# Turning probabilities in two halves of the array's rows, and an opening in which the products of w3 and w_out reach over steps 0 to 3

## The chip, the core and the metric

One core of one Trainium2 chip runs the kernel. Its engines run side by side, each through its own queue in order: TensorE (PE, with PEld for its loads of weights), VectorE (DVE), ScalarE (ACT), GpSimd (POOL) and SyncE (SP), which issues the DMAs. The metric is device time in microseconds (us), lower is better.

## What is computed

Banded attention with a few global keys, and a feed-forward part on its output:

```python
# attention, 4 batches, 8 heads, 768 positions, head size 64, n_global = 8, n_local = 96
scores = q @ k.T / 8 + bias        # bias = -slope(head) * distance
keep = (key < n_global) | ((0 <= row - key) & (row - key < n_local))
a = softmax(where(keep, scores, -1e9))
x = (a @ v) laid out as 3072 x 512
# feed-forward: w1, w2 are 512 x 1024, w3 is 1024 x 1024, w_out is 1024 x 512
out = (((x @ w1) * (x @ w2)) @ w3) @ w_out
```

The weights arrive as 64-bit numbers and are turned to 32 bits on the chip.

## The kernel before

**Steps.** The 4 batches are cut into 12 column blocks `c` of 256 positions, the 8 heads into 4 pairs. A step `s` handles two pairs of heads of one block; there are 24 steps, two for each `c`. A block that begins a batch (`c` divisible by 3: steps 0, 1, 6, 7, 12, 13, 18, 19) has less to do, and is called *first* here; the other steps are *full*.

- `visit(s)`: TensorE makes the values of step s-1 (`values`, L468) and the scores of step s (`scores`, L405), both in tiles of 64 rows by 64 columns of the array. Values go to two tiles `uu` of the pool `ps_v`, which has two PSUM banks. ScalarE copies one (L503), VectorE adds the other (L504), and the sum is split into a high and a low part, `xh` on ScalarE (L63) and `xl` on VectorE (L64).
- `rows` (L420, L421): VectorE adds the bias and finds the extreme of each row, ScalarE takes exp, eight times a step. `softmax` (L426 to L435) divides by the sum; in the opening ScalarE does all eight scalings (`scale(s)`, L433), and this call also issues the loads of step s+1 (`loads`, `qr` and `vr`).
- `turn(s, i)` for the two pairs: TensorE transposes the probabilities through the same two banks (`flip`, L445, L447), ScalarE copies each bank out to `ph` (L449, an *eviction*).
- `FeedForward.run`: the feed-forward of one stretch of x, as a generator. One call of `slices(1)` runs it to its next `yield`. The function takes a width: the first two blocks are run at 256 columns each, all later ones in pairs at 512. A slice is six matmuls of 512 columns, or twelve of 256. A pair of blocks at 512 takes 48 slices (32 for w1 and w2, L161 to L163, 16 for the product, L178 to L180); a single block at 256 takes 16 + 8.

**The opening.** w3 and w_out are multiplied once at the start: `fold(f, k...)` (L142), eight products for each of the eight blocks `f` of w3, each product two matmuls of 512 columns; then `low(f)` (L147) takes the low part of the sum. `w3(f)` and `w12(f)` bring a block of w3, or of w1 and w2: two DMAs into staging tiles, a conversion of three VectorE operations each (`convert`, L54, L56, L58), for w1 and w2 a copy on ScalarE (L122) and a low part on VectorE (`lows`, L130). The staging tile `raws` holds two pieces, `stage` four.

**What sets the order.** TensorE runs in the order of the code. In `first_steps` VectorE and SP do so as well, and the scheduler places ScalarE; in the later steps ScalarE is in code order and the scheduler places the other two. `SLICES` says how many slices stand ahead of, between and behind the two turnings of a step: (4, 4, 2) in steps 3 to 5, (4, 2, 2) in 6 and 7, (5, 4, 3) from 8 on. So 46 of the first 48 slices have run when step 8 begins.

Of the kernel before, what the change touches and what calls it, by code (L numbers as in the profile page):

```python
# [10 lines left out]
F32 = mybir.dt.float32  # L11
# [9 lines left out]
P = 128  # L21
# [45 lines left out]
class FeedForward:  # L67
# [29 lines left out]
    def weights(self, *names):  # L97
# [3 lines left out]
        for kind, *at in names:  # L101
            if kind == "w":
                f, n = divmod(at[0], 2)

                raw = self.stage[{3: 0, 5: 2, 6: 0}[f] + n] if f in (3, 5, 6) else self.raws[:, n]
                dst, src = self.t3s[:, at[0] % 4], self.src[n][f]
                fresh.append((n, f, dst.bitcast(F32).rearrange("p (i m) -> p i m", i=NCC)))
            elif kind == "o":
                dst, src = self.wo[:, at[0]], self.w_out[at[0]]
            else:  # L110
                f, z = at
                dst = self.mp.tile([P, PC], I32, tag=self.next(0, "agagoo"), name=f"t3_{f}_{z}")
                src = self.w3t[f, :, z * PC:(z + 1) * PC]
                self.t3[f, z] = dst
# [210 lines left out]
def banded(ctx, tc, ff, ns, nt, nf, oki, ident, qk, vx):  # L325
# [111 lines left out]

    def flip(c, hp, j, pr):

        first = c % NCB == 0 and j == 0  # L440
        nk = 1 if first else 2

        pt = ps_v.tile([P, 2, 2, P], F32, tag="v", name=f"t_{c}_{hp}_{j}")
        for u in range(2):
            nc.tensor.transpose(pt[:, u, 0], pr[:, j, u, BW:UW], ident)  # L445
            if not first:
                nc.tensor.transpose(pt[:, u, 1], pr[:, j, u, 0:P], ident)  # L447
        ph = at.tile([P, 2, 2, P], F32, tag="ph", bufs=4, name=f"ph_{c}_{hp}_{j}")
        nc.scalar.activation(ph[:, :, :nk], pt[:, :, :nk], AF.Copy)  # L449
        return ph  # L450

    def values(uu, c, hp, vr, phs):


        lo, hi, both = slice(0, HQ), slice(HQ, P), slice(0, P)
        for j, ph in enumerate(phs):
            own, win = (j, 0), (2 * NQ - 1 - j, 1)
            if c % NCB == 0 and j == 0:
                seqs = [[(own, r, both, True, True)] for r in (lo, hi)]
            else:  # L460
# [3 lines left out]
            for parts in zip(*seqs):  # L464
                for u in range(2):
                    rows = slice(u * D, (u + 1) * D)
                    for r, ((i, k), keys, q, start, stop) in enumerate(parts):
                        nc.tensor.matmul(uu[r][rows, j * P:][:, q], lhsT=vr[keys, i, rows], rhs=ph[keys, u, k, q], start=start, stop=stop)  # L468

# [20 lines left out]
    def visit(s):  # L490
        if s:
# [4 lines left out]
            for i, p in enumerate(pairs(s - 1)):  # L496
                values([x[:, i] for x in uu], *p, vrs[s - 1][i], phs[s - 1][NQ * i:NQ * (i + 1)])
        ps = [scores(*p, t) for p, t in zip(pairs(s), qrs[s])] if s < n else []
        if s:
# [5 lines left out]
            split(nc, *(x[:, h0:h0 + STEP] for x in xc), v)  # L505
            if h0 + STEP == NP and c < 2:
                work.append(ff.run(c, *xc, c * T, T))
            elif h0 + STEP == NP and c % 2:
                work.append(ff.run(c, *x2, (c - 1) * T, W))
# [5 lines left out]
    def turn(s, i, prs):  # L515

        phs.setdefault(s, []).extend(flip(*pairs(s)[i], j, prs[i][0]) for j in range(NQ))

    def first_steps():
# [43 lines left out]

        def fold_and_turn(f, s):
            ff.fold(f, 0, 1, 2, 3)
            turn(s, 0, prs)
            ff.fold(f, 4, 5, 6)
            turn(s, 1, prs)
            ff.fold(f, 7)

        w3(3)
        scale(0)
        ff.low(0)
        w3(4)
        ff.low(1)
        ff.low(2)
        w3(5)
        w12(0)
        fold_and_turn(3, 0)
        ff.lows()  # L580
        w3(6)
# [24 lines left out]
        prs = all_rows(3, visit(3))
        w12(6)
        slices(2)
        scale(3)
        ff.lows()  # L610
        w12(7)
        slices(SLICES[3][0] - 2)
        ff.lows()
        for i in range(STEP):
            turn(3, i, prs)
            slices(SLICES[3][i + 1])
        fits(nc, ff.mp, nf, oki)


    SLICES = [()] * 3 + [(4, 4, 2)] * 3 + [(4, 2, 2)] * 2 + [(5, 4, 3)] * (n - 8)  # L620
    with tc.manual_schedule(engines={mybir.EngineType.PE}):
        with tc.manual_schedule(engines={mybir.EngineType.DVE, mybir.EngineType.SP}):
            first_steps()
        with tc.manual_schedule(engines={mybir.EngineType.Activation}):
            for s in range(4, n + 1):
                rs = all_rows(s, visit(s))
# [6 lines left out]
                loads(s + 1)  # L633
                slices(SLICES[s][0] - 2)
                for i in range(STEP):
                    turn(s, i, rs)
                    slices(SLICES[s][i + 1])
            slices(10 ** 6)
# [45 lines left out]
```

## Time and profile before

| | |
|---|---|
| median of 3 runs | 591.76 us (591.63 to 592.16) |
| the profiled execution | 591.84 us |
| its span, first to last instruction | 589.8 us |
| TensorE busy | 565.4 us, 96% of the span |
| ScalarE busy | 297.3 us, 50% |
| VectorE busy | 274.2 us, 46% |
| mean granted clock of TensorE | 0.993 |
| share of TensorE in the chain that ended last | 82% (VectorE 13%, ScalarE 2%, DMA 2%) |

Matmuls overlap in the records, so the mean duration of one is longer than the time between the starts of two; for TensorE the document goes by starts.

### The profile page before, as it was taken

What the parts mean: (1) busy time and instruction counts of PE and PEld (TensorE: products, weight loads), DVE (VectorE), ACT (ScalarE), POOL (GpSimd) and SP (SyncE); (2) the same over time, 40 slices, a digit from 0 to 9 for tenths busy, and PEclk for the clock granted to TensorE, in tenths of its full rate; (3) what the DMA queues carried; (4) which work ended last, traced back from release to release, by engine and by line L of the source; (5) the groups of instructions that cost most, each with busy time, mean ns of one, the idle gap of its engine ahead of it and who ended that gap; (6) DMA issues with size and microseconds to landing.
All of it is one profiled execution on the core that took longest, in us unless ns stands there. A gap on an engine that the chain in (4) does not pass through costs nothing.

```text
span 589.8 us, 12652 instructions
## 1 busy us (share of the span) xinstructions
PE 565.4 (96%) x5216; PEld 452.0 (77%) x5216; DVE 274.2 (46%) x875; ACT 297.3 (50%) x801; POOL 1.3 (0%) x10
## 2 busy tenths in 40 slices
PE   2998996999999999999999999999999999999995
PEld 0444556989988888888888888888888888888884
DVE  8999999524444445404534432552244354022200
ACT  3065688446666456536646545663555565322210
POOL 0000000000000000000000000000000000000000
PEclk9999997999999999999999999999999999999999
DMA  8896754202223202212210330221232020100001
GB/s 300 306 359 239 224 217 148 82 21 82 65 80 116 67 15 81 64 55 82 81 57 24 102 114 18 66 64 35 82 116 79 2 82 1 54 19 1 0 36 41
DMA packets 23252, 54.19 MB, mean 92 GB/s; under 512 B 2705, under 2 KB 4753, under 8 KB 23185
## 3 DMA queue, kind: packets, MB, share of 16 engines
q1 hardware_dynamic: 23184, 53.29, 26.6%
q8 instruction: 43, 0.70, 0.5%
q14 instruction: 25, 0.20, 0.1%
HBM read 46.99 MB, written 6.29 MB: 90 GB/s over the span
## 4 chain that ended last, share of the span: by engine, by line
PE 82%; DVE 13%; ACT 2%; DMA 2%; issue 1%; DVEq 0%; ACTq 0%
PE m L161 15%; PE m L162 15%; PE m L163 15%; PE o L178 8%; PE o L179 7%; PE o L180 7%; PE v L468 5%; PE s L405 4%; PE t L445 3%; PE t L447 3%; DVE pr L420 2%; DVE t L58 1%; DVE t L56 1%; DVE t3s L56 1%; DMA stage<-w3t 1%; DVE t3s L58 1%
## 5 line engine op out<-in xcount | busy, mean ns | idle before, releaser
L421 ACT ACTIVATE pr<-pr,mx 128x232 f32<-128x232 f32 (+1 forms) x192 | 88.3, 461 | 23.4 <-DVE mx L420 21.6
L171 DVE TENSOR_TENSOR g<-m,a 128x512 f32<-128x512 f32 x48 | 33.0, 687 | 132.0 <-PE m L163 128.6
L161 PE MATMUL m<-xh,w2h 128*128 128x512 f32 (+1 forms) x224 | 84.4, 377 | 0.0
L161 PE MATMUL m<-xh,w1h 128*128 128x512 f32 (+1 forms) x224 | 81.6, 364 | 0.0
L162 PE MATMUL m<-xl,w1h 128*128 128x512 f32 (+1 forms) x224 | 81.0, 362 | 0.0
L163 PE MATMUL m<-xh,w1l 128*128 128x512 f32 (+1 forms) x224 | 81.0, 361 | 0.0
L162 PE MATMUL m<-xl,w2h 128*128 128x512 f32 (+1 forms) x224 | 80.8, 361 | 0.0
L163 PE MATMUL m<-xh,w2l 128*128 128x512 f32 (+1 forms) x224 | 80.7, 360 | 0.0
L178 PE MATMUL o<-wh,gh 128*128 128x512 f32 x192 | 77.0, 401 | 0.0
L179 PE MATMUL o<-wl,gh 128*128 128x512 f32 x192 | 75.1, 391 | 0.0
L180 PE MATMUL o<-wh,gl 128*128 128x512 f32 x192 | 74.9, 390 | 0.0
L142 PE MATMUL w<-wo,t 128*128 128x512 f32 x128 | 60.6, 623 | 13.1 <-DVE wo L58 11.1
L449 ACT ACTIVATE ph<-t 128x512 f32<-128x512 f32 (+1 forms) x96 | 49.8, 557 | 44.2 <-PE t L447 29.5
L504 DVE TENSOR_TENSOR vs<-v,vs 128x512 f32<-128x512 f32 x24 | 16.6, 690 | 117.2 <-ACT vs L503 117.2
L63 ACT ACTIVATE gh<-g 128x512 fp32r<-128x512 f32 x48 | 30.3, 630 | 68.1 <-DVE g L171 68.1
L142 PEld LDWEIGHTS w<-wo,t 128*128 128x128 f32 x128 | 24.3, 198 | 42.5 <-issue 24.2
L420 DVE CUSTOM_DVE_ANT_0 pr<-s,biasw 128x232 f32<-128x232 f32 x160 | 54.9, 394 | 0.0
L168 ACT ACTIVATE a<-m 128x512 f32<-128x512 f32 x48 | 28.4, 591 | 45.0 <-PE m L163 45.0
L161 PEld LDWEIGHTS m<-xh,w2h 128*128 128x128 f32 x224 | 42.3, 189 | 8.7 <-issue 2.6
L161 PEld LDWEIGHTS m<-xh,w1h 128*128 128x128 f32 x224 | 43.0, 192 | 6.6 <-DVE t3s L58 0.2
L445 PE MATMUL t<-ident,pr 128*128 128x128 f32 x192 | 43.0, 278 | 5.3 <-ACT pr L433 5.2
L162 PEld LDWEIGHTS m<-xl,w1h 128*128 128x128 f32 x224 | 43.0, 192 | 6.4
(84 smaller groups left out, 800.5 us busy)
## 6 DMA issues: line engine op xcount, KB each, us to landing
qr<-qk SPq DMA_DIRECT2D x32, 312.0 KB, 4.4
vr<-vx SPq DMA_DIRECT2D x32, 256.0 KB, 3.5
stage<-w3t SPq DMA_DIRECT2D x15, 512.0 KB, 6.8
out_dram<-ot SPq DMA_DIRECT2D x24, 256.0 KB, 2.0
raws<-w SPq DMA_DIRECT2D x10, 512.0 KB, 6.1
qr<-qk SPq DMA_DIRECT2D x16, 260.0 KB, 4.1
vr<-vx SPq DMA_DIRECT2D x16, 192.0 KB, 3.7
stage<-w SPq DMA_DIRECT2D x6, 512.0 KB, 7.1
```

The costliest lines, as they stand in the source:

```text
L142: nc.tensor.matmul(ps, lhsT=self.t3[f, z][:, i * P:(i + 1) * P].bitcast(F32), rhs=self.wo[:, k].bitcast(F32), start=k == 0, stop=k == NFC - 1)
L161: nc.tensor.matmul(ps[:, z], lhsT=mh, rhs=xh[:, i], start=i == 0, stop=False)
L162: nc.tensor.matmul(ps[:, z], lhsT=mh, rhs=xl[:, i], start=False, stop=False)
L163: nc.tensor.matmul(ps[:, z], lhsT=ml, rhs=xh[:, i], start=False, stop=i == NCC - 1)
L171: nc.vector.tensor_tensor(out=g, in0=ps, in1=a, op=ALU.mult)
L178: nc.tensor.matmul(ps, lhsT=gh[:, f, ts], rhs=self.wh[:, f], start=f == 0, stop=False)
L179: nc.tensor.matmul(ps, lhsT=gh[:, f, ts], rhs=self.wl[:, f], start=False, stop=False)
L180: nc.tensor.matmul(ps, lhsT=gl[:, f, ts], rhs=self.wh[:, f], start=False, stop=f == NFC - 1)
L420: nc.vector.tensor_tensor_reduce(out=pr[:, j, u, w0:], in0=ps[u][:, j, w0:UW], in1=bias, scale=-SCALE, scalar=3.0e38, op0=ALU.add, op1=ALU ...
L421: nc.scalar.activation(pr[:, j, u, w0:], pr[:, j, u, w0:], AF.Exp, bias=m, scale=-1.0, accum_out=sm[:, j, u:u + 1])
L445: nc.tensor.transpose(pt[:, u, 0], pr[:, j, u, BW:UW], ident)
L449: nc.scalar.activation(ph[:, :, :nk], pt[:, :, :nk], AF.Copy)
```

## The change

Two things change together.

**Turning.** `flip` now handles a whole pair of heads. Each transpose of 128 by 128 becomes two of 64 rows, one in the upper and one in the lower half of the array's rows (tiles of 64 rows by 128 columns), with 64 moving columns each, into two tiles of `ps_v`, one for each half. So each tile holds half of the positions of both `j`. An eviction is still 128x512, or 128x128 and 128x256 where the step is a first one; `values` picks the tile by the half that it needs, and its only 128-column matmuls are cut in two.

**Opening.** The first two blocks are run as a pair at 512 columns like the others, so the first slices come in step 4 instead of step 3. The products of w3 and w_out are spread by hand around the turnings of steps 0 to 3 (`around`), the conversions of w1 and w2 come later, and their staging tiles are dealt anew. Steps 4 to 7 now have 10, 12, 12 and 12 slices, again 46 of 48 when step 8 begins.

```diff
@@ weights @@
-                raw = self.stage[{3: 0, 5: 2, 6: 0}[f] + n] if f in (3, 5, 6) else self.raws[:, n]
+                raw = self.stage[{2: 0, 4: 2, 5: 0}[f] + n] if f in (2, 4, 5) else self.raws[:, n]
@@ flip @@
-        pt = ps_v.tile([P, 2, 2, P], F32, tag="v", name=f"t_{c}_{hp}_{j}")
-        for u in range(2):
-            nc.tensor.transpose(pt[:, u, 0], pr[:, j, u, BW:UW], ident)
-            if not first:
-                nc.tensor.transpose(pt[:, u, 1], pr[:, j, u, 0:P], ident)
-        ph = at.tile([P, 2, 2, P], F32, tag="ph", bufs=4, name=f"ph_{c}_{hp}_{j}")
-        nc.scalar.activation(ph[:, :, :nk], pt[:, :, :nk], AF.Copy)
+        halves = [slice(g * HQ, (g + 1) * HQ) for g in range(2)]
+        pts = [ps_v.tile([P, NQ, 2, 2, HQ], F32, tag="v", name=f"t{g}_{c}_{hp}") for g in range(2)]
+        for j in range(NQ):
+            for u in range(2):
+                for k, cols in enumerate((slice(BW, UW), slice(0, P))[:1 if first and j == 0 else 2]):
+                    for q, pt in zip(halves, pts):
+                        nc.tensor.transpose(pt[:, j, u, k], pr[q, j, u, cols], ident[q, q])
+        phs = [at.tile([P, NQ, 2, 2, HQ], F32, tag="ph", bufs=4, name=f"ph{g}_{c}_{hp}") for g in range(2)]
+        for ph, pt in zip(phs, pts):
+            if first:
+                nc.scalar.activation(ph[:, 0, :, 0], pt[:, 0, :, 0], AF.Copy)
+                nc.scalar.activation(ph[:, 1], pt[:, 1], AF.Copy)
+            else:
+                nc.scalar.activation(ph, pt, AF.Copy)
@@ visit @@
-            if h0 + STEP == NP and c < 2:
-                work.append(ff.run(c, *xc, c * T, T))
-            elif h0 + STEP == NP and c % 2:
+            if h0 + STEP == NP and c % 2:
                 work.append(ff.run(c, *x2, (c - 1) * T, W))
@@ later steps @@
-    SLICES = [()] * 3 + [(4, 4, 2)] * 3 + [(4, 2, 2)] * 2 + [(5, 4, 3)] * (n - 8)
+    SLICES = (5, 4, 3)
-            for s in range(4, n + 1):
+            for s in range(5, n + 1):
```

The new order in `first_steps`, behind `w3(3)`, `scale(0)` and `ff.low(0)`:

```python
ff.low(2)
w3(4)
ff.low(1)
around(0, [(3, 0, 1)], [(3, 2, 2)], [(3, 3, 4)])
w3(5)
prs = all_rows(1, visit(1))
ff.fold(3, 5, 6, 7)
ff.weights(("w", 0))
ff.low(3)
scale(1)
ff.weights(("w", 1))
around(1, [(4, 0, 4)], [(4, 5, 5)], [(4, 6, 7)])
ff.lows()
w3(6)
prs = all_rows(2, visit(2))
ff.low(4)
scale(2)
w12(1)
around(2, [(5, 0, 7), (6, 0, 0)], [(6, 1, 1)], [(6, 2, 3)])
ff.lows()
ff.low(5)
w3(7)
w12(2)
prs = all_rows(3, visit(3))
ff.lows()
scale(3)
w12(3)
around(3, [(6, 4, 7), (7, 0, 3)], [(7, 4, 5)], [(7, 6, 7)])
ff.lows()
ff.low(6)
w12(4)
ff.lows()
ff.low(7)
prs = all_rows(4, visit(4))
w12(5)
slices(2)
scale(4)
ff.lows()
slices(SLICES[0] - 2)
w12(6)
turn(4, 0, prs)
slices(2)
ff.lows()
slices(SLICES[1] - 2)
w12(7)
turn(4, 1, prs)
slices(SLICES[2] - 2)
ff.lows()
```

`around(s, a, b, e)` runs the products of list `a`, the first turning of step s, list `b`, the second turning, list `e`; (3, 0, 1) stands for the products 0 to 1 of block 3.

How the built programs differ, at three places. On TensorE, the first turning of step 0: `w_360` and `w_340` are the sums of block 3, `pr` the probabilities, `t` the tile they are turned into. Before:

```order
L142 MATMUL w_360<-wo,t_3_0_297 128x512 x4
L445 MATMUL t_0_0_365<-ident,pr_0_266 128x128 x2
L445 MATMUL t_0_1_370<-ident,pr_0_266 128x128
L447 MATMUL t_0_1_370<-ident,pr_0_266 128x128
L445 MATMUL t_0_1_370<-ident,pr_0_266 128x128
L447 MATMUL t_0_1_370<-ident,pr_0_266 128x128
L142 MATMUL w_360<-wo,t_3_1_298 128x512 x3
```

and after:

```order
L142 MATMUL w_340<-wo,t_3_0_297 128x512 x2
L448 MATMUL t_0_0_343<-ident,pr_0_266 128x64
L448 MATMUL t_0_0_344<-ident,pr_0_266 128x64
L448 MATMUL t_0_0_343<-ident,pr_0_266 128x64
L448 MATMUL t_0_0_344<-ident,pr_0_266 128x64
...
L142 MATMUL w_340<-wo,t_3_0_297 128x512
```

Six transposes into one tile after the other became twelve that alternate between two tiles, and two of the products ahead of the turning moved behind it. On VectorE, after the softmax of step 0: `w_168`, `w_180` and `w_182` are the sums of blocks 0, 1 and 2, the last in a bank of `ps_v`. Before:

```order
L427 RECIPROCAL sm_1_279<-sm_1_279 128x4
L147 TENSOR_TENSOR wl<-w_168,wh 128x512
L54 TENSOR_SCALAR t_4_0_328<-stage 128x512
L54 TENSOR_SCALAR t_4_1_329<-stage 128x512
```

and after:

```order
L427 RECIPROCAL sm_1_279<-sm_1_279 128x4
L147 TENSOR_TENSOR wl<-w_168,wh 128x512
L147 TENSOR_TENSOR wl<-w_182,wh 128x512
L54 TENSOR_SCALAR t_4_0_329<-stage 128x512
L54 TENSOR_SCALAR t_4_1_330<-stage 128x512
```

The low part of block 2, which stood behind the conversion of block 4, now stands ahead of it. On SP, the loads of step 3 (`qr_2`, `qr_3`, `vr_2`, `vr_3`) and the DMAs of `w12(1)` into `raws`. Before:

```order
L50 DMA stage<-w3t 128x1024 x2
L50 DMA raws<-w 128x1024 x2
L50 DMA stage<-w 128x1024 x2
L383 DMA qr_2_695<-qk 128x624
L383 DMA qr_3_697<-qk 128x624
L390 DMA vr_2_699<-vx 128x512
```

and after:

```order
L383 DMA qr_2_678<-qk 128x624
L383 DMA qr_3_680<-qk 128x624
L390 DMA vr_2_682<-vx 128x512
L390 DMA vr_3_684<-vx 128x512
L50 DMA raws<-w 128x1024 x2
L50 DMA stage<-w3t 128x1024 x2
```

The loads of step 3, which stood behind the DMAs of two blocks of w1 and w2 (f = 2 into `raws`, f = 3 into `stage`), now stand ahead of those of f = 1.

On ScalarE, the two turnings of step 2, before and after: the copies of a block of w1 and w2 (`w1h`, `w2h`) stand between the evictions of the first and of the second turning. After:

```order
L455 ACTIVATE ph_1_0_726<-t_1_0_708 128x512
L455 ACTIVATE ph_1_0_727<-t_1_0_709 128x512
L122 ACTIVATE w1h<-t3s 128x512
L122 ACTIVATE w2h<-t3s 128x512
L455 ACTIVATE ph_1_1_749<-t_1_1_731 128x512
```

In that place they are those of f = 1; before the change they were those of f = 4.

## Rows read from the trace of the kernel before

**Rows 1.** The page: TensorE's busy time, share and instructions; and VectorE's busy share in 40 equal slices of the span, in tenths.

```profile
PE 565.4 (96%) x5216; PEld 452.0 (77%) x5216; DVE 274.2 (46%) x875; ACT 297.3 (50%) x801; POOL 1.3 (0%) x10
...
DVE  8999999524444445404534432552244354022200
```

**Rows 2.** Sums over stretches of time: length, busy time of TensorE, PEld, VectorE, ScalarE and GpSimd (instructions), granted TensorE clock, DMA share, GB/s.

```profile
130.00:514.00 384.00, 384.00 (x3929) 322.47 (x3930) 152.24 (x566) 213.43 (x585) 0.00 (x0) 1.00 0.20 65
...
98.00:104.00 6.00, 5.58 (x29) 5.45 (x30) 5.16 (x10) 5.55 (x13) 0.00 (x0) 0.56 0.01 3
```

**Rows 3.** Timeline of TensorE around the last values (no scores follow them): start, duration, line, tiles and shape, count. The first and second row are the first and the last of five matmuls of 512 columns in a row.

```profile
512.71 0.39 PE L179 MATMUL o<-wl,gh 128*128 128x512 f32 x1
...
513.62 0.39 PE L180 MATMUL o<-wh,gl 128*128 128x512 f32 x1
513.94 1.63 PE L468 MATMUL v<-ph,vr 64*64 64x64 f32 x96
...
515.83 0.39 PE L179 MATMUL o<-wl,gh 128*128 128x512 f32 x1
```

**Rows 4.** Timeline of TensorE, a full turning (eight transposes) and the visit that follows it.

```profile
126.44 0.27 PE L445 MATMUL t<-ident,pr 128*128 128x128 f32 x1
126.55 0.27 PE L447 MATMUL t<-ident,pr 128*128 128x128 f32 x1
...
127.55 0.40 PE L179 MATMUL o<-wl,gh 128*128 128x512 f32 x1
...
129.82 0.39 PE L180 MATMUL o<-wh,gl 128*128 128x512 f32 x1
130.14 1.63 PE L468 MATMUL v<-ph,vr 64*64 64x64 f32 x96
131.59 1.32 PE L405 MATMUL s<-qr 64*64 64x168 f32 x32
...
133.19 0.40 PE L179 MATMUL o<-wl,gh 128*128 128x512 f32 x1
```

**Rows 5.** Timeline of TensorE, two matmuls of 256 columns in a row.

```profile
142.20 0.28 PE L161 MATMUL m<-xh,w2h 128*128 128x256 f32 x1
142.32 0.28 PE L162 MATMUL m<-xl,w2h 128*128 128x256 f32 x1
```

**Rows 6.** Groups of loads of weights by line and shape: count, busy time, mean ns of one, idle time of PEld before them.

```profile
L163 PEld LDWEIGHTS m<-xh,w1l 128*128 128x128 f32 x224 | 42.9, 192 | 6.2
...
L468 PEld LDWEIGHTS v<-ph,vr 64*64 64x64 f32 x1408 | 33.5, 134 | 9.0 <-issue 6.3 <-ACT ph L449 2.3
...
L445 PEld LDWEIGHTS t<-ident,pr 128*128 128x128 f32 x192 | 26.6, 141 | 13.0 <-ACT pr L433 8.2 <-issue 1.6 <-ACT ph L449 0.2
```

**Rows 7.** Timeline of VectorE in the opening: the conversion of two pieces (first and following operation), the softmax, a low part, the values' sum, and the eight row operations of a full step (first row, and the conversion behind them).

```profile
31.58 0.76 DVE L54 TENSOR_SCALAR t<-stage 128x512 int32<-128x512 int32 x2
...
34.66 0.16 DVE L426 TENSOR_SCALAR sm<-sm 128x4 f32<-128x4 f32 x1
...
35.22 0.66 DVE L147 TENSOR_TENSOR wl<-w,wh 128x512 fp32r<-128x512 f32 x1
35.80 0.42 DVE L54 TENSOR_SCALAR t<-stage 128x512 int32<-128x512 int32 x1
...
51.66 0.68 DVE L504 TENSOR_TENSOR vs<-v,vs 128x512 f32<-128x512 f32 x1
...
53.64 0.28 DVE L420 CUSTOM_DVE_ANT_0 pr<-s,bias 128x128 f32<-128x128 f32 x1
...
71.92 0.39 DVE L420 CUSTOM_DVE_ANT_0 pr<-s,biasw 128x232 f32<-128x232 f32 x1
...
74.47 0.76 DVE L54 TENSOR_SCALAR t3s<-stage 128x512 int32<-128x512 int32 x2
```

**Rows 8.** Timeline of ScalarE in the opening: the high part of block 2's sum, the scalings of a first step, the last exp of a full step, the scalings of a full step, two evictions.

```profile
37.27 0.58 ACT L144 ACTIVATE wh<-w 128x512 fp32r<-128x512 f32 x1
...
60.09 2.79 ACT L433 ACTIVATE pr<-pr,sm 128x128 f32<-128x128 f32 x8
...
75.67 0.47 ACT L421 ACTIVATE pr<-pr,mx 128x232 f32<-128x232 f32 x1
...
78.69 3.13 ACT L433 ACTIVATE pr<-pr,sm 128x232 f32<-128x232 f32 x8
81.72 1.06 ACT L449 ACTIVATE ph<-t 128x512 f32<-128x512 f32 x2
```

**Rows 9.** Timeline of TensorE in the opening: 32 matmuls of the products, six more between two turnings, and the first turning of step 3 with its idle time in front.

```profile
26.55 14.00 PE L142 MATMUL w<-wo,t 128*128 128x512 f32 x32
...
41.25 2.74 PE L142 MATMUL w<-wo,t 128*128 128x512 f32 x6
43.83 0.49 PE L445 MATMUL t<-ident,pr 128*128 128x128 f32 x3
...
98.42 0.47 PE L445 MATMUL t<-ident,pr 128*128 128x128 f32 x1 [4.67 <-ACT pr L433]
```

**Rows 10.** Timeline of SP, two loads of `qr` and two DMAs into `raws` behind them.

```profile
87.32 1.00 SPq L383 DMA_DIRECT2D qr<-qk  x2
...
89.36 0.85 SPq L50 DMA_DIRECT2D raws<-w  x2
```

**Rows 11.** The ten DMAs into `raws`, from issue to landing.

```profile
DMA to landing us min/median/max: 3.6/6.1/8.8
```

More of the change, by code (lines that the diff above doesn't have):

```diff
@@ L436, in softmax, with flip @@
         return pr
-    def flip(c, hp, j, pr):
-        first = c % NCB == 0 and j == 0
-        nk = 1 if first else 2
-        pt = ps_v.tile([P, 2, 2, P], F32, tag="v", name=f"t_{c}_{hp}_{j}")
-        for u in range(2):
-            nc.tensor.transpose(pt[:, u, 0], pr[:, j, u, BW:UW], ident)
-            if not first:
-                nc.tensor.transpose(pt[:, u, 1], pr[:, j, u, 0:P], ident)
-        ph = at.tile([P, 2, 2, P], F32, tag="ph", bufs=4, name=f"ph_{c}_{hp}_{j}")
-        nc.scalar.activation(ph[:, :, :nk], pt[:, :, :nk], AF.Copy)
-        return ph
+    def flip(c, hp, pr):
+        first = c % NCB == 0
+        halves = [slice(g * HQ, (g + 1) * HQ) for g in range(2)]
[12 more added lines that the diff above has]
+                nc.scalar.activation(ph, pt, AF.Copy)
+        return phs
     def values(uu, c, hp, vr, phs):
-        lo, hi, both = slice(0, HQ), slice(HQ, P), slice(0, P)
-        for j, ph in enumerate(phs):
+        lo, hi = slice(0, HQ), slice(HQ, P)
+        for j in range(NQ):
             own, win = (j, 0), (2 * NQ - 1 - j, 1)
             if c % NCB == 0 and j == 0:
-                seqs = [[(own, r, both, True, True)] for r in (lo, hi)]
+                seqs = [[(own, r, q, True, True) for q in (lo, hi)] for r in (lo, hi)]
             else:
@@ L467, in values @@
                     for r, ((i, k), keys, q, start, stop) in enumerate(parts):
-                        nc.tensor.matmul(uu[r][rows, j * P:][:, q], lhsT=vr[keys, i, rows], rhs=ph[keys, u, k, q], start=start, stop=stop)
+                        nc.tensor.matmul(uu[r][rows, j * P:][:, q], lhsT=vr[keys, i, rows], rhs=phs[q is hi][keys, j, u, k], start=start, stop=stop)
     n = NC * NP // STEP
@@ L496, in visit @@
             for i, p in enumerate(pairs(s - 1)):
-                values([x[:, i] for x in uu], *p, vrs[s - 1][i], phs[s - 1][NQ * i:NQ * (i + 1)])
+                values([x[:, i] for x in uu], *p, vrs[s - 1][i], phs[s - 1][i])
         ps = [scores(*p, t) for p, t in zip(pairs(s), qrs[s])] if s < n else []
@@ L515, in turn @@
     def turn(s, i, prs):
-        phs.setdefault(s, []).extend(flip(*pairs(s)[i], j, prs[i][0]) for j in range(NQ))
+        phs.setdefault(s, []).append(flip(*pairs(s)[i], prs[i][0]))
     def first_steps():
@@ L562, in scale, with around @@
             loads(s + 1)
[L564 to L569, printed above, removed]
+        def around(s, a, b, e):
+            for i, part in enumerate((a, b, e)):
+                for f, k0, k1 in part:
+                    ff.fold(f, *range(k0, k1 + 1))
+                if i < STEP:
+                    turn(s, i, prs)
         w3(3)
@@ L633, in banded @@
                 loads(s + 1)
-                slices(SLICES[s][0] - 2)
+                slices(SLICES[0] - 2)
                 for i in range(STEP):
                     turn(s, i, rs)
-                    slices(SLICES[s][i + 1])
+                    slices(SLICES[i + 1])
             slices(10 ** 6)
```

37 lines of the change are left out of this document (14 added, 23 removed).

## Prediction

> **What bounds the kernel now.** The busy times come first: TensorE is busy 96% of the span, and VectorE's tenths stand at 9 for the first seven slices of forty, then at about 4 [rows 1]. The sums by stretch sharpen it: from 130 to 514 us TensorE is busy all the time at full clock [rows 2]. So the kernel has two parts. Up to the visit of step 5 (its values start at 130.14 [rows 4]) VectorE's conversions keep TensorE waiting, for instance 4.67 us ahead of the first turning of step 3 [rows 9]; behind it, only the amount of TensorE's work counts, and the profiled execution needs 589.8 - 130.1 = 459.7 us for it. I work out when the same visit starts after the change, and what is left then.
>
> **Unit prices.** A 512-column matmul starts 0.2275 us after the one before it (four in 0.91 us [rows 3]), a slice of six takes 1.36; a 256-column one 0.12 [rows 5]; a product of w3 and w_out 0.86 (six matmuls in 2.58 [rows 9]). A visit takes 1.45 for the values and 1.37 for the scores with what follows (131.59 to 133.19, less one matmul [rows 4]). VectorE: a conversion of two pieces 3.08, a softmax 0.56, a low part 0.6, from the sum of the values to the rows 1.98, the eight rows of a full step 2.55 [rows 7]. ScalarE: its last exp ends 4.2 us after the rows began (75.67 + 0.47, against 71.92 [rows 7, 8]); eight scalings take 3.03 in a full step and 2.7 in a first one, an eviction 0.5 [rows 8].
>
> **The turning.** Eight transposes with the start of the next matmul take 1.11 us (126.44 to 127.55), less one matmul 0.88: 0.11 each and nothing lost at the edges [rows 4]; a first turning has six, 0.66. After the change eight pairs of half transposes take their place. What a pair costs no row shows. Half the moving columns would be 0.055 a pair if both halves run side by side. Values are 64-column matmuls in four tiles: 96 in 1.45 us, four in 0.060 [rows 4], so loads and matmuls of different row halves do overlap. I take r = 0.058, between the two; the upper bound is 0.109, if a load sets the pace.
>
> Edges are the second cost. Entering the values costs 0.32 - 0.23 = 0.09 (513.62 to 513.94), leaving them 0.21 (513.94 to 515.83 is 1.89, less 1.45, less one matmul), together 0.30 where the tile shape changes both ways [rows 3]; between full-size transposes and matmuls it is nothing. The halves are tiles of another shape, so I charge 0.30 a turning; the lower bound is 0, if only column tiles pay. A full turning then costs 8 x 0.058 + 0.30 = 0.76 instead of 0.88, a first one 0.65 instead of 0.66. Steps 5 to 23 have 26 full and 12 first turnings: 26 x 0.116 + 12 x 0.012 = 3.2 us saved; in general 19.4 - 280 r. The Trainium skill, page "TensorEngine Tiling (Array Packing)", section Key Properties, says that a change of tiling mode drains TensorE, whichever mode it is; by it the 0.30 stands and the 0 falls away, and the rows show it for 64x64 tiles alone.
>
> Evictions keep their number; a first turning's four smaller pieces cost ScalarE some 0.4 us more, hidden by three or four slices (4 to 5 us) before a bank is needed again. Both banks are now needed at once, and both are free by then, for the same reason. The cut values matmuls cost nothing: eight of 64 columns for four of 128.
>
> **The width of the first two blocks.** 384 matmuls at 0.12 become 192 at 0.2275: 46.1 - 43.7 = 2.4 us saved. At the visit of step 5 the old kernel has run 20 narrow slices of the pair's 48, the new one 10 wide ones. Left of the pair: 16 x 1.44 + 12 x 1.36 = 39.4 before, 38 x 1.36 = 51.7 now, so 12.3 more behind that visit, and the opening has to win it back.
>
> **The opening, step by step.** Up to 35.8 us the program stands as before.
> - *Step 0.* The low part of block 2 moves ahead of the conversion of block 4. It needs the high part that ScalarE ends at 37.85 [rows 8], so VectorE waits 2.0 us, and conversions 4 and 5 end at 41.6 and 45.2. TensorE: the 24 matmuls of products 4 to 7 of blocks 0 to 2 end at 26.55 + 24 x 0.43 = 36.9 [rows 9], then five products and two turnings, the second waiting for both evictions of the first (40.5). Visit 1 starts at 42.9.
> - *Step 1.* Visit and eight products last to 52.3. VectorE adds the values at 45.2, rows 47.2 to 49.3, one piece of w1 to 51.2, low part 52.2, softmax 52.8; ScalarE scales until 55.4, then evicts. The second turning waits for that until 56.6. Visit 2 starts at 58.9. VectorE waits 2 us for w2's copy, which stands behind those evictions.
> - *Step 2.* Nine products to 69.2. The DMAs of w12(1) stand on SP behind the loads of step 3, which wait for the scores of step 2 (first pair some 0.8 us after their start at 60.2). `raws` is issued 2.0 us after the first `qr` [rows 10], at 63.1, and 6.1 later [rows 11] both pieces have landed by about 69.7. Conversion to 72.7, copies to 73.9, then the second turning's evictions, to 74.9: visit 3, where TensorE alone would be ready at 74.0.
> - *Step 3.* VectorE: low parts, w3(7), w12(2) to 81.3; the split of the values waits on ScalarE behind w12(2)'s copies, so rows run 83.2 to 85.8, exps to 87.4, scalings to 91.0. TensorE has eight products until 84.6 and then waits until 89.5 for the first turning; the second waits for a bank whose eviction stands behind w12(3)'s copies, to 93.2. Visit 4 starts at 96.1. The idle 4 us may lower the clock as in the old step 3 (granted 0.56 from 98 to 104 us, mostly the lower level, 1.2 GHz [rows 2]); the bank sets the time there, so it costs under 1 us.
> - *Step 4.* The values' sum stands on VectorE behind w12(4); xl is ready at 101.0, and TensorE waits 2 us for its first slice. Five slices, a turning that waits for scalings until 109.3, four slices, a turning, one slice; evictions behind w12(6)'s copies. **Visit 5 starts at 117.0**, 13.1 earlier than before.
> - *Step 5.* w12(7) uses `raws` again, issued when w12(6) is converted (114.8), and is converted by 121.6; the rows of step 5 stand behind it, and the first turning waits until 130.6 where 127.4 was possible: 3.2 us lost.
>
> Sum: 117.0 + 3.2 + 459.7 + 12.3 - 3.2 = 589.0 us of span, and 589.0 + 2.0 = 591.0 for the execution (591.84 lies 2.04 over its span). The median of the runs lies 0.1 under the profiled one: **590.9**. The opening gains 13.1 and gives back 12.3 and 3.2; the turnings save 3.2. This is no change to within 0.2%, which is what a measurement of this kernel can tell. My chain has some twelve hops, each good to about half a us, so this case alone spans 586 to 596.
>
> **Rivals.**
> - *Edges are free for row halves.* For it: both shapes keep 128 columns. Against: every change of shape in the trace pays. 38 turnings x 0.30 = 11.4 less: **579.5**.
> - *A half transpose pays a whole load (slower).* Place: PEld in each turning. If a load of 64 rows and 128 columns takes as long as the old transpose, a pair takes 0.109 and the halves save nothing but pay the edges: 280 x 0.051 = 14.3 more, **605**. The whole becomes slower by over 0.2% from r of 0.065. Against it: loads of 128 columns for the feed-forward record 192 ns, those of 64 columns 134, and those of a transpose, 128 columns, only 141 [rows 6]; if 64 columns more cost 58 ns, a transpose's 128, only 7 ns over a record of 64, take some 65 ns, and side by side like the values' loads. The Trainium skill, page "TensorE: Matmul & The Clock Gate", section LDWEIGHTS, has this rival as a rule: a load costs by its columns, not its rows, an estimate of 107 ns for 128 at its 1.2 columns a ns. By it the sum would be 605; the trace agrees for the 58 ns between 64 and 128 columns, not for the transposes' 141.
> - *VectorE never waits in the opening.* Its queue from 31.6 to the end of the rows of step 4 sums to 62 us (conversions 31.3, eighteen low parts 10.8, sums and rows 17.7, softmaxes 2.2), so these could end at 93.6 instead of 103.6; visit 5 would start 10 earlier: **581**. Against: seven waits on ScalarE, each in the built order.
> - *More waits than I found*, say of step 6 on the same ring: up to 5 us more, inside the first case's range.
>
> **How the numbers follow.** First case 0.60, free edges 0.16, whole load 0.16, no waits 0.08. No change means 590.6 to 592.9. Since a hop that I missed can only delay, I give the first case 0.42 below that, 0.22 in it and 0.36 above. Faster: 0.60 x 0.42 + 0.16 + 0.08 = 0.49; same: 0.60 x 0.22 = 0.13; slower: 0.60 x 0.36 + 0.16 = 0.38. The range takes in free edges and leaves out the whole load and 4 in 100 of the first case: 578.5 to 600.
>
> **What would show it.** In the new trace: the start of the values of step 5 near 117, TensorE idle near 85 to 89 and 99 to 101, VectorE waiting near 36 for `wh`; in steady steps 1.0 us from the first half transpose to the second matmul behind it (0.69 if edges are free, 1.40 if a load sets the pace). I am wrong if the visit of step 5 starts before 113 or after 121, or if that distance is not near 1.0.

## The result and the profile after

The changed kernel takes **596.86 us** (median of 4 runs, 594.96 to 598.45), the one before 591.73 on the same chip: ratio 1.0085 (1.0069 to 1.0100), slower by 0.85%. The profiled execution is the fastest of the four, 594.96 us with a span of 593.2. The predicted span was 589.0, so 4.2 us have to be explained in this execution, and what the others take on top.

The page's busy line and VectorE's tenths [rows 1]: TensorE has hardly more to do, and VectorE's 9s are broken up.

```profile
PE 565.6 (95%) x5504; PEld 428.1 (72%) x5504; DVE 273.9 (46%) x871; ACT 300.3 (51%) x837; POOL 1.3 (0%) x10
...
DVE  8998798774333245414524423542333454022200
```

Timeline of TensorE: visits 4, 5, 6, 8 and 24 (starts of values), the turnings and waits of steps 3 and 5, and at 198 us a full turning with the matmul ahead of it and two behind [rows 3, 4, 9].

```profile
87.55 1.62 PE L448 MATMUL t<-ident,pr 64*128 64x64 f32 x16 [3.75 <-ACT pr L433]
...
94.76 1.63 PE L474 MATMUL v<-ph,vr 64*64 64x64 f32 x96
...
116.18 1.63 PE L474 MATMUL v<-ph,vr 64*64 64x64 f32 x96
...
127.14 0.50 PE L161 MATMUL m<-xh,w2h 128*128 128x512 f32 x1 [2.49 <-DVE g L171]
...
128.97 1.12 PE L448 MATMUL t<-ident,pr 64*128 64x64 f32 x16
...
141.57 0.64 PE L474 MATMUL v<-ph,vr 64*64 64x64 f32 x28
...
182.68 1.40 PE L474 MATMUL v<-ph,vr 64*64 64x64 f32 x80
...
198.38 0.39 PE L163 MATMUL m<-xh,w2l 128*128 128x512 f32 x1
198.70 0.71 PE L448 MATMUL t<-ident,pr 64*128 64x64 f32 x16
199.34 0.50 PE L161 MATMUL m<-xh,w2h 128*128 128x512 f32 x1
199.68 0.40 PE L162 MATMUL m<-xl,w2h 128*128 128x512 f32 x1
...
517.29 1.63 PE L474 MATMUL v<-ph,vr 64*64 64x64 f32 x96
```

Visit 8 of the kernel before, where both kernels have 46 slices behind them; its visit 24 is at 513.94 [rows 3].

```profile
179.43 1.37 PE L468 MATMUL v<-ph,vr 64*64 64x128 f32 x64
```

So nearly the whole loss is made by visit 8: 182.68 against 179.43, 3.25 us, and at visit 24 it is 3.35. From 8 to 24 the changed kernel needs 334.61 us, the one before 334.51: **the halves save nothing there**, where 2.9 of the forecast 3.2 should have come.

VectorE: its two waits for `raws` in step 2; then, in step 5, the conversion of w12(7), the first row behind it, and g, for which TensorE waits at 127.14.

```profile
68.19 0.43 DVE L54 TENSOR_SCALAR t3s<-raws 128x512 int32<-128x512 int32 x1 [1.22 <-DMA raws<-w]
69.44 0.43 DVE L54 TENSOR_SCALAR t3s<-raws 128x512 int32<-128x512 int32 x1 [0.82 <-DMA raws<-w]
...
118.49 1.31 DVE L56 SCALAR_TENSOR_TENSOR t3s<-raws,t3s 128x512 int32<-128x512 int32 x2
119.69 1.31 DVE L58 SCALAR_TENSOR_TENSOR t3s<-raws,t3s 128x512 int32<-128x512 int32 x2
...
123.06 0.41 DVE L420 CUSTOM_DVE_ANT_0 pr<-s,biasw 128x232 f32<-128x232 f32 x1
...
126.41 0.68 DVE L171 TENSOR_TENSOR g<-m,a 128x512 f32<-128x512 f32 x1
```

Sums over stretches (length, busy TensorE, PEld, VectorE, ScalarE, GpSimd, granted clock, DMA share, GB/s), first of the kernel after, then of the one before. The first two stretches are at the lower level of the clock, 1.2 GHz; they begin behind waits of TensorE of 3.75 and 2.49 us.

```profile
87.65:91.06 3.41, 3.41 (x19) 1.94 (x20) 2.46 (x5) 3.41 (x10) 0.00 (x0) 0.50 0.35 135
128.61:132.03 3.42, 3.32 (x22) 2.56 (x22) 1.33 (x4) 3.00 (x7) 0.00 (x0) 0.50 0.00 0
...
30.00:98.00 68.00, 62.21 (x689) 32.47 (x689) 57.56 (x160) 48.02 (x145) 0.00 (x0) 0.97 0.63 223
```

```profile
30.00:98.00 68.00, 61.59 (x505) 34.26 (x503) 64.32 (x175) 45.49 (x130) 0.00 (x0) 0.99 0.72 254
```

From 30 to 98 us VectorE is idle for 10.4 us after the change and for 3.7 before. It comes to the last conversion at 118 us instead of 99, which is this row of the kernel before:

```profile
98.98 0.76 DVE L54 TENSOR_SCALAR t3s<-raws 128x512 int32<-128x512 int32 x2
```

### The profile page after: what moved, and what is told of

Read it like the earlier page. It is cut to its first block, busy times and chain, and to the rows that moved or that the text cites. A ratio compares the mean times of both kernels' runs of the same rounds, so it can differ in the third digit from the quotient of the medians.

```text
span 593.2 us, 13276 instructions
## 1 busy us (share of the span) xinstructions
PE 565.6 (95%) x5504; PEld 428.1 (72%) x5504; DVE 273.9 (46%) x871; ACT 300.3 (51%) x837; POOL 1.3 (0%) x10
## 4 chain that ended last, share of the span: by engine, by line
PE 78%; DVE 13%; ACT 5%; DMA 2%; issue 1%; ACTq 0%; DVEq 0%
PE m L161 15%; PE m L162 14%; PE m L163 14%; PE o L178 8%; PE o L179 7%; PE o L180 7%; PE v L474 5%; PE t L448 4%; PE s L405 3%; DMA raws<-w 2%; ACT pr L421 2%; ACT pr L433 2%; DVE t L56 1%; DVE t L58 1%; DVE t3s L56 1%; DVE pr L420 1%
## 5 line engine op out<-in xcount | busy, mean ns | idle before, releaser
L161 PE MATMUL m<-xh,w2h 128*128 128x512 f32 x192 | 80.3, 418 | 2.5 <-DVE g L171 2.5
L161 PE MATMUL m<-xh,w1h 128*128 128x512 f32 x192 | 75.5, 393 | 0.9 <-ACT a L168 0.6
L162 PE MATMUL m<-xl,w2h 128*128 128x512 f32 x192 | 75.6, 394 | 0.0
L163 PE MATMUL m<-xh,w2l 128*128 128x512 f32 x192 | 75.3, 392 | 0.0
L162 PE MATMUL m<-xl,w1h 128*128 128x512 f32 x192 | 74.9, 390 | 0.2 <-DVE xl L64 0.2
L180 PE MATMUL o<-wh,gl 128*128 128x512 f32 x192 | 74.9, 390 | 0.0
L163 PE MATMUL m<-xh,w1l 128*128 128x512 f32 x192 | 74.8, 389 | 0.0
L455 ACT ACTIVATE ph<-t 128x512 f32<-128x512 f32 x64 | 34.7, 594 | 32.0 <-PE t L448 32.0
L448 PEld LDWEIGHTS t<-ident,pr 64*128 64x128 f32 x704 | 27.5, 141 | 28.5 <-ACT pr L433 13.6
L64 DVE TENSOR_TENSOR gl<-g,gh 128x512 fp32r<-128x512 f32 x48 | 33.2, 691 | 28.5 <-ACT gh L63 28.1
L433 ACT ACTIVATE pr<-pr,sm 128x232 f32<-128x232 f32 (+1 forms) x116 | 44.8, 461 | 0.7 <-DVE sm L426 0.6
```

Source lines behind the costliest of these rows:

```text
L161: nc.tensor.matmul(ps[:, z], lhsT=mh, rhs=xh[:, i], start=i == 0, stop=False)
L162: nc.tensor.matmul(ps[:, z], lhsT=mh, rhs=xl[:, i], start=False, stop=False)
L163: nc.tensor.matmul(ps[:, z], lhsT=ml, rhs=xh[:, i], start=False, stop=i == NCC - 1)
L180: nc.tensor.matmul(ps, lhsT=gl[:, f, ts], rhs=self.wh[:, f], start=False, stop=f == NFC - 1)
L433: nc.scalar.activation(x, x, AF.Copy, scale=r)
L448: nc.tensor.transpose(pt[:, j, u, k], pr[q, j, u, cols], ident[q, q])
```

## The experiments

The code of each change is shortened below. The theory at this point: the halves are break-even, and the opening costs 3 to 4 us because VectorE waits more in it. The rivals: two banks needed at once delay the opening; what costs is in the order of ScalarE and TensorE; the slower executions have other waits.

| run | median us | ratio to before (95%) |
|---|---|---|
| e1 halves only | 592.82 | 1.0022 (1.0012 to 1.0031) |
| e2 opening only | 595.26 | 1.0059 (1.0042 to 1.0076) |
| e3 changed kernel again | 595.57 | 1.0081 (1.0057 to 1.0105) |
| e4 w12 early | 596.87 | 1.0084 (1.0063 to 1.0105) |
| e5 loads behind | 595.29 | 1.0057 (1.0042 to 1.0073) |
| e6 step 5 slices | 599.09 | 1.0124 (1.0101 to 1.0146) |
| e7 full turnings, e5 and e6 | 599.12 | 1.0117 (1.0103 to 1.0132) |
| e8 halves in a row | 604.85 | 1.0212 (1.0198 to 1.0227) |
| e9 before, light | 585.76 | 0.9883 (0.9862 to 0.9904) |
| e10 after, light | 588.36 | 0.9934 (0.9914 to 0.9953) |
| e11 halves in late full steps | 591.37 | 0.9991 (0.9981 to 1.0001) |
| e12 scale first | 591.95 | 1.0005 (0.9996 to 1.0014) |
| e13 e11 and e12 | 591.41 | 0.9996 (0.9987 to 1.0005) |

Starts of some visits in the profiled executions, us:

| visit | before | after | e1 | e2 | e3 | e4 | e5 | e6 | e7 | e9 | e10 | e11 | e12 | e13 |
|---|---|---|---|---|---|---|---|---|---|---|---|---|---|---|
| 4 | 111.14 | 94.76 | 111.96 | 96.15 | 96.30 | 96.85 | 96.10 | 95.79 | 93.03 | 105.11 | 92.31 | 110.05 | 110.62 | 110.41 |
| 5 | 130.14 | 116.18 | 130.89 | 117.30 | 117.63 | 122.39 | 117.71 | 117.22 | 117.35 | 124.15 | 113.51 | 129.10 | 130.98 | 130.78 |
| 6 | 148.92 | 141.57 | 149.60 | 142.13 | 142.28 | 143.61 | 142.46 | 144.48 | 146.14 | 142.95 | 135.11 | 147.89 | 149.76 | 149.55 |
| 8 | 179.43 | 182.68 | 180.40 | 182.93 | 183.39 | 184.72 | 183.57 | 185.59 | 186.94 | 173.46 | 176.22 | 178.40 | 180.27 | 180.06 |
| 24 | 513.94 | 517.29 | 515.01 | 517.32 | 518.02 | 519.33 | 518.16 | 520.20 | 521.39 | 507.96 | 510.83 | 512.31 | 514.77 | 513.96 |

**The two parts apart.** e1 is the kernel before with the new `flip` and `values`, e2 the changed kernel with the old ones.

```diff
 e1: -    def flip(c, hp, j, pr):      (old opening kept)
     +    def flip(c, hp, pr):
 e2: -    def flip(c, hp, pr):         (new opening kept)
     +    def flip(c, hp, j, pr):
```

> The opening of before, with the turnings in halves. Theory (the halves are break-even, the opening costs): a full turning saves 0.04 us and a first one costs 0.06, so 26 x 0.041 - 12 x 0.056 = 0.4 us less behind step 4, and up to 1 us more in the opening, where the second turning must now wait for two banks: 591.3 to 592.6, granted clock low only in the two stretches of before. Rival A (the need for two banks at once delays the opening): 594 or more, and the visit of step 5 starts over 2 us later than 130.1. Rival B (the halves save what was forecast and only the opening eats it): 588.5.

> The new opening, with the full-size turnings of before. Theory: the loss stays, 0.4 us more than the changed kernel: profiled 595.4, median about 597, spread of some 3 us between executions, visit of step 5 near 116, that of step 8 near 183. Rival A (two banks at once are what costs): 593 or less, and the waits at the second turnings of steps 0 to 3 shorter. Rival B: 600, with each full turning 0.12 longer.

The shares add: 0.22% and 0.59% against 0.81 and 0.85% for both. e1's theory holds for the opening (0.75 us lost by visit 5, where up to 1 was forecast), but the 0.4 us that it expected to gain behind step 4 didn't come: 334.61 us from visit 8 to 24, as after the change, and a time 0.2 us above its range. Rival A is there but small: the timeline of e1 shows new waits for the banks.

```profile
40.76 0.59 PE L448 MATMUL t<-ident,pr 64*128 64x64 f32 x11 [0.67 <-DVE wl L147]
...
83.99 0.27 PE L448 MATMUL t<-ident,pr 64*128 64x64 f32 x1 [0.18 <-ACT ph L455]
84.48 0.71 PE L448 MATMUL t<-ident,pr 64*128 64x64 f32 x15 [0.21 <-ACT ph L455]
```

e2 keeps some 70% of the loss without any halves, so that part belongs to the opening. Its median is 1.7 us below the forecast 597: it was expected a little above the changed kernel and lies below it. Rival B is out for both.

**The changed kernel again.**

> The changed kernel once more, for its spread. Theory: the executions differ by where the granted clock falls in the opening and in step 5, where TensorE waits 2 to 4 us; a slower execution than the first profiled one has one or two more stretches of 3.4 us at 0.50, each worth up to 1.7 us, and the same waits otherwise. Median 596 to 598. Rival: the clock falls at the same places and the difference is in the waits for DMAs (weights that land later).

Four executions at 594.76 to 595.85 us have mean granted clocks of 0.995 or 0.996, the two at 598.50 and 598.77 have 0.985 and 0.987. So a lower mean clock goes with the longest times, as the theory had it; where it fell in them isn't shown, since only the first has a trace, and the rival (later landings) is not tested. The median is 0.4 us below the forecast. This one has no low stretch in step 5, as the fastest had, and is still 0.7 us later at visit 8, as it already is at visit 1 (42.93 against 42.17): early delays count too.

**Step 5.** e4 takes the conversions out of the way of its rows, e6 gives TensorE more slices ahead of the turning.

```diff
 e4: -        w12(5); slices(2); scale(4); ff.lows(); slices(SLICES[0] - 2); w12(6); turn(4, 0, prs)
     +        w12(5); scale(4); w12(6); slices(2); ff.lows(); slices(SLICES[0] - 2); w12(7); turn(4, 0, prs)
 e6: -                rs = all_rows(s, visit(s)); slices(2); ...
     +                ps = visit(5); slices(2); rs = all_rows(5, ps); ... cut 8, 2, 2
```

> The changed kernel, with the DMAs of w12(6) in the staging tiles of w12(4) and the conversions of w12(6) and w12(7) ahead of the slices and of the first turning of step 4, so that none stands ahead of the rows of step 5. Theory (step 5 loses 4.7 us since the conversion of w12(7) stands ahead of its rows): from the visit of step 5 to that of step 6 takes 20.7 instead of 25.4 us, TensorE doesn't wait for g, no clock fall there; step 4 pays up to 2 us of it back: 592 to 595. Rival (the scheduler's order in step 5, g behind eight rows, makes the wait): the wait for g stays over 2 us, and the time at 596 or more.

> The changed kernel, with the first two slices of step 5 ahead of its rows in the order, so that g stands ahead of most rows on VectorE, and the 12 slices of step 5 cut 8, 2, 2 around its turnings instead of 5, 4, 3. Theory (step 5 loses 4 to 4.7 us since the rows start only when w12(7) is converted, and only five slices stand ahead of the turning that needs them): the slices cover it, TensorE doesn't wait for g, from visit 5 to visit 6 takes 21 to 21.5 us instead of 24.7 to 25.4, and the time is 592 to 593. Rival (two slices between the turnings are too few for the evictions, and the banks of the second turning come late): 23 to 24 us for the step, 594 to 595.

e4: step 5 takes 21.2 us, near the forecast 20.7, but step 4 now 25.5 instead of 21.4, where up to 2 more was allowed for; the two together 46.76 against 46.81, and the time lies where the rival had it, though the rival's wait for g in step 5 is gone. The loss has moved whole: the copies of w12(6) and w12(7) and eight scalings now stand ahead of `a` on ScalarE, and a stretch of low clock (3.41 us at 0.50, from 115.69) follows the wait. TensorE in e4:

```profile
114.23 0.50 PE L161 MATMUL m<-xh,w2h 128*128 128x512 f32 x1 [2.44 <-ACT a L168]
```

e6 missed both forecasts, 27.3 us for the step, with a stretch of low clock in it (3.41 us at 0.50, from 133.51, behind the second wait below). A slice needs a bank that ScalarE (`a`) and VectorE (g) have emptied, so slices can't cover a wait while the exps hold ScalarE:

```profile
126.29 0.50 PE L161 MATMUL m<-xh,w2h 128*128 128x512 f32 x1 [0.60 <-DVE g L171]
132.73 0.50 PE L161 MATMUL m<-xh,w1h 128*128 128x512 f32 x1 [3.40 <-ACT a L168]
```

**VectorE's wait for raws.**

```diff
 e5: -        scale(2)              (softmax of step 2, loads(3))
     -        w12(1)
     +        softmax of step 2
     +        w12(1)
     +        loads(3)
```

> The changed kernel, with the loads of step 3 issued on SP behind the DMAs of w12(1) instead of ahead of them. Theory (VectorE is the bound up to step 5, and what it waits there comes back at the end): its wait of 2.0 us for raws at 68 us goes, the wait of TensorE ahead of the first turning of step 3 falls from 3.8 to about 2, visit 4 starts 1.5 to 2 us earlier, and the time is 593.5 to 594.5. Rival (the wait only moves: the copies on ScalarE or the turning's banks are next): visit 4 within 0.5 of 94.8 to 96.3, time 595 to 596.5.

> Full-size turnings with the new opening, and both edits of e5 and e6. Theory: the two losses are of different steps and add, 595.3 - 1.7 - 3.5 = 590.1, below the kernel before (591.7). Rival (VectorE's and ScalarE's chain is one, so that one edit's gain is the other's wait): 592 or more.

In e5 the wait of 2.0 us is gone and that of TensorE ahead of step 3's first turning fell to 2.02, but the second turning of step 2 waits 1.46 for its eviction, and visit 4 starts where it did in e2 and e3 (a stretch of low clock at 56 us had cost this execution 1 to 2 us before that). The time is within the spread of the changed kernel, where the rival had it. The two waits of e5:

```profile
73.69 0.27 PE L448 MATMUL t<-ident,pr 64*128 64x64 f32 x1 [1.46 <-ACT ph L455]
...
88.58 1.48 PE L448 MATMUL t<-ident,pr 64*128 64x64 f32 x16 [2.02 <-ACT pr L433]
```

e7 shows why a gain at visit 4 need not last: there visit 4 starts at 93.03, 3 us earlier than in e2, and visit 5 at 117.35 as in e2. TensorE and VectorE of e7 in step 4:

```profile
100.65 0.49 PE L161 MATMUL m<-xh,w1h 128*128 128x512 f32 x1 [3.20 <-ACT xh L63]
```

```profile
95.68 1.27 DVE L58 SCALAR_TENSOR_TENSOR t3s<-stage,t3s 128x512 int32<-128x512 int32 x2
...
99.26 0.68 DVE L504 TENSOR_TENSOR vs<-v,vs 128x512 f32<-128x512 f32 x1
```

The values' sum stands behind w12(4) on VectorE and starts at 99.26, though TensorE had begun the values at 93.03; what TensorE won it waits off, and a stretch of low clock (3.41 us at 0.50) follows at 101.58. The two edits don't add (the rival): 599.12 instead of 590.1. Step 5 takes 28.8 us, so e6's part costs here too.

**Do the halves run side by side?**

```diff
 e8: -        for j ...: for u ...: for k ...: for q, pt in zip(halves, pts): transpose
     +        for q, pt in zip(halves, pts): for j ...: for u ...: for k ...: transpose
```

> The opening of before with turnings in halves as in e1, but first all transposes of the lower half of the rows, then all of the upper, instead of alternating. Theory (the two halves run side by side, starts 4 ns apart, a pair each 62 ns): in a row each half transpose takes 55 to 62 ns by itself, so a full turning is 8 x 0.06 longer and a first one 6 x 0.06: 26 x 0.48 + 12 x 0.36 = 16.8 more than e1, about 609. Rival (a half transpose takes 31 ns whatever stands beside it, half a full one's time of half the work): no change to e1, 592.8.

12.0 us more than e1, so they do, and the rival is out. A full turning:

```profile
243.12 0.39 PE L163 MATMUL m<-xh,w2l 128*128 128x512 f32 x1
243.44 1.02 PE L448 MATMUL t<-ident,pr 64*128 64x64 f32 x16
244.38 0.50 PE L161 MATMUL m<-xh,w2h 128*128 128x512 f32 x1
```

From its start to the next matmul 0.94 us against 0.64 in turns. Transposes of one half start 62 ns apart while none of the other half runs, so this is the price of one, alone or in a pair. The forecast was 16.8 because it had no overlap left; in the single records of this turning the upper half's first transpose starts 0.30 us behind the lower half's first, while three of the lower half are still to come.

**With VectorE light.** The second operation of `convert` (L56, sign and top bit of the exponent) is left out in both kernels, so weights and output are others.

```diff
 e9, e10:
-        nc.vector.scalar_tensor_tensor(out=dst, in0=w[:, :, 1], scalar=-0x40000000, ...)
```

> The kernel before, with one of the three VectorE operations of each conversion left out (the one that puts in the sign and the top bit of the exponent, so the weights, and the output, are others): 0.6 us less of VectorE for each of 40 pieces, 12 us of them between 31 and 103 us. Theory (up to step 5 the chain through VectorE sets the time): TensorE's idle time in the opening goes, 6.9 us of idle and some 3 of low clock there: 581 to 586.

> The changed kernel with the same operation left out of each conversion (other weights and output, as in the run before this one). Theory (the new opening loses since VectorE, which waits 10 us between 30 and 98 us instead of 3, comes to the last conversion too late): with VectorE light it gains more than the old one, 10 us of idle and 2 to 3 of low clock, and lies at or below the light kernel before, by up to 2.8 us (2.4 for the width, 0.4 for the turnings): 579 to 584. Rival (what costs is on TensorE and ScalarE: two banks at once, copies and evictions in each other's way): it stays 3 or more above the light kernel before.

Both fall. e9 is in its range, e10 is 4 us above its own. Between them are 0.51% instead of the 0.83% of the full kernels (the mean of 0.85 and 0.81), but each pair is good to some 0.2 to 0.3%, so whether e10 gained more than e9 isn't clear of noise. In step 5 it is clear: the step takes 21.6 us in e10, so its loss was VectorE's. In exchange the lead over the old opening at visit 5 falls from 13.96 us to 10.64 (124.15 - 113.51), since the old opening gains 6.0 us there from the lighter conversions too. So e10 doesn't pass e9, and neither theory has it whole: TensorE of e10 waits for evictions at two banks, as the rival says.

```profile
71.34 0.27 PE L446 MATMUL t<-ident,pr 64*128 64x64 f32 x1 [2.33 <-ACT ph L453]
72.35 0.71 PE L446 MATMUL t<-ident,pr 64*128 64x64 f32 x15 [0.73 <-ACT ph L453]
```

**A better version?** e11 keeps full-size turnings except in the 24 of full steps from step 8 on; e12 edits the old opening; e13 is both.

```diff
 e11: +        if first or c < 4: full-size turning
 e12: -        w12(6); slices(2); scale(3); ff.lows(); w12(7); slices(SLICES[3][0] - 2); ff.lows()
      +        slices(2); scale(3); w12(6); slices(SLICES[3][0] - 2); ff.lows(); w12(7); ff.lows()
```

> The kernel before, with halves only in the full steps from step 8 on (24 turnings), full-size turnings everywhere else. Theory (a full turning in halves saves 0.04 us, a first one costs 0.06 and the opening's two banks cost 0.75): 24 x 0.04 = 1.0 us less than before, 590.8, each full step 0.06 to 0.08 shorter. Rival (the halves cost in full steps too): 591.7 or more.

> The kernel before, with the scalings of step 3 ahead of the conversion of w12(6), and g ahead of that of w12(7), on VectorE. Theory (what sets the opening is what stands ahead of the rows and scalings in VectorE's and ScalarE's queues, not how much TensorE has to do): the wait of 4.7 us ahead of the first turning of step 3 falls to about 2.5, visit 4 starts 1.5 to 2.5 us earlier, with it the end: 589.2 to 590.2. Rival (the wait moves to the second turning or to the slices of step 3, whose g and a come later): 591 or more.

> The same, with halves in the 24 full turnings from step 8 on, as in e11. Theory: the two gains are of different parts and add, 0.4 to 0.6 us less than e12, 588.7 to 589.7, the best of all. Rival (e11's gain over before was chance in its opening): equal to e12, and the stretch from visit 8 to visit 24 is 334.5 as before instead of 333.9.

From visit 8 to 24 e11 takes 333.91 and e13 333.90, where before and e12 take 334.51 and 334.50: 24 turnings save 0.60 us, 0.025 each, where 1.0 was forecast. In the whole time that is at the edge of what can be measured, and neither is shown to be faster than the kernel before; the forecasts of 590.8 (e11), 589.2 to 590.2 (e12) and 588.7 to 589.7 (e13) were all missed. e12's wait fell from 4.67 to 3.09 us, less than forecast, and step 4 became 1.4 us longer (20.36 against 19.00): its rows now stand behind w12(7) on VectorE, and its first turning waits for the scalings.

```profile
120.73 0.33 PE L445 MATMUL t<-ident,pr 128*128 128x128 f32 x1 [1.40 <-ACT pr L433]
```

This execution had also lost 1 us by visit 2, in a stretch of low clock at 57 us; e13, which has none there, shows the same 20.4 us for step 4. So the wait moved here too, as the rival said, though to the next step.

## Why the prediction was wrong

Its sum missed by 4.2 us of span, 593.2 against 589.0. One term makes 3.6 of it; the others nearly cancel.

- **The saving of the turnings, 3.2 us, was mis-sized: it is a loss of 0.4.** From visit 8 on nothing is saved (-0.1); steps 5 to 7 would take 62.16 us undisturbed (steps 10, 12 and 13 of the changed kernel) and 61.89 with full-size turnings (steps 15, 18, 19 of before). Over the 24 full turnings from step 8 on, the time from the start of the matmul ahead to that of the second one behind is 1.299 us (198.38 to 199.68 above) against 1.340, in the 8 first ones 1.176 against 1.118 (medians of the starts). Taking off two matmuls, 0.845 where 0.76 was forecast, 0.72 where 0.65. Both prices were low: the pair is 0.062, not 0.058; the edges are 0.35, not 0.30: 0.09 to enter (198.38 to 198.70, less a matmul) and, behind the last pair, 0.09 to the next matmul and 0.11 to the second, and a first pair of 0.113, 0.05 above the others. These errors, 0.085 in 26 full turnings and 0.07 in 12 first ones, are 3.0 of the 3.6 us. Most of the rest lies behind the second matmul: of the 0.041 that a full turning saves up to there, the whole step keeps 0.025 to 0.03 (a step with two takes 21.05 us against 21.11). In first steps the six pairs don't pay for the edges: from e11 to the changed kernel the 8 first turnings from step 8 on and their cut values cost 0.70 us. The cut values, taken to cost nothing, are some 0.03 of it in each of five visits (1.40 in place of 1.37 at visit 8 above).
- **The missing 0.05 could be read before the change.** In the trace of the kernel before, the first four matmuls of a visit's values take 0.108 us and the next fours 0.058 (medians of the starts). The prediction spread 1.45 us over 96 matmuls, which hides the dearer first four in the price of 0.060, and then charged the edge without them.
- **The signs that were named passed, and yet were no test.** Visit 5 at 116.18 is between 113 and 121. "1.0 us from the first half transpose to the second matmul behind it" is 0.98. But that stretch leaves out the entry, which lies ahead of the first transpose; the forecast's own prices without it give 0.90 (8 x 0.058 + 0.21 + one matmul), so the match was luck.
- **The loss in step 5 was 4.3 us, not 3.2** (25.39 against 21.05 in an undisturbed step of 12 slices). The wait was forecast at the first turning; it came at the slice ahead of it, for g, which stands behind all eight rows on VectorE. e2 and e3 lose 3.7 and 3.6 there without a low clock; the stretch of low clock at 128.6 us, which the prediction didn't expect, would be the rest, though no run tests it alone. The cause of the loss, w12(7) ahead of the rows, is shown by e4, which moves the loss with the conversion, and e10 agrees (0.5 lost when VectorE is light).
- **In one sum, against the kernel before:** the changed kernel leads by 13.96 us at visit 5, has 12.60 more left behind it, loses 4.34 in step 5 and 0.34 in turnings: 3.3 us later at the end. By this sum it would be 1.0 ahead without the loss in step 5; no run reached that.
- **The chain through the opening was right.** Forecast visits 42.9, 58.9, 74.9, 96.1, 117.0; measured 42.17, 58.10, 73.65, 94.76, 116.18. The wait for `raws` (2.0 us) and TensorE's ahead of step 3's first turning (3.75) came where they were said to come; the idle time "99 to 101" was 0.6 us, not 2. Visit 5 came 0.8 early, and the work left behind visit 5 was counted 0.3 short: 3.6 + 1.1 + 0.3 - 0.8 = 4.2.
- **The range was about right, the point not.** Of the rivals, "no waits" and "free edges" were wrong outright, and so was "more waits" for step 6: steps 6 and 7 take 41.11 us, as steps 12 and 13. "A whole load" was wrong too, with 0.062 for 0.109. But its remark that an r of 0.065 already turns the sign was the warning to heed: with the forecast's 0.30 for the edges, 0.845 a turning is an r of 0.068. The Trainium skill's page "TensorEngine Tiling (Array Packing)", section Key Properties, has a change of mode drain TensorE: the trace agrees for 64x128 tiles, where entering takes 0.09 us and leaving 0.20. The rule of the Trainium skill's page "TensorE: Matmul & The Clock Gate", section LDWEIGHTS, would have given 107 ns a pair (an estimate from its rate); the transposes of this trace don't follow it, with 62 ns.
- **The median was taken to lie where the profiled execution lies.** It lies 1.9 us above it in the first four runs, and with that 6.0 above the forecast 590.9. The mean clock is lower in the longest of them (0.991 at 594.96, 0.987 at 598.45); what lowers it from one execution to the next is not shown.

What stays open is which hops make the new opening's 0.59%. In the traces the loss in step 5 is as large as all of it, and that loss is VectorE's; but light conversions take it away without making the new opening the faster one, and whether they narrow the gap at all (0.51 against 0.83%) isn't clear of noise. Two banks at once delay the opening as well (0.75 us by visit 5 in e1). Each single wait that was removed came back at the next queue, and no order was found that frees all three engines.

## What to carry to other kernels

A change that halves a group's work but alters the tile shape has to pay for entering and leaving; count the instructions in a group at which the two meet (here between seven and eight pairs: 0.35 over 0.047), and don't forecast a sign on either side of it without a row for the edge itself, the dearer first instruction included. Where several engines hand a chain on to each other, the end of a wait is worth something only if the next engine's queue is free by then; look up what stands there before crediting it. A sign that is to test a term must hold the whole term, entry included.

## What the runs showed of the hardware

- A transpose of 64 rows and 128 columns takes 62 ns behind another of the same half, and one in the other half of the rows starts 4 ns beside it; one of 128 rows takes 109 ns. With all of one half ahead of all of the other in the code (e8), the second half's first still starts while three of the first half's are to come, so TensorE's own queue, said above to run in order, doesn't start everything strictly in that order.
- The first pair of a group takes 113 ns, about as long as a full-size transpose. The values show the same (0.108 us for their first four, 0.058 for later ones), and in e8 the first transpose of each half does: 111 ns, for the second half as well, though no change of shape lies just ahead of it. Why is not shown.
- Executions of one program differed by up to 4.0 us (594.76 to 598.77), and the mean granted clock with them: 0.995 at the one, 0.987 at the other.
